# Chunked gated linear attention: one decay reference per 128-token chunk in place of one per 64-token half, and small matmuls cut to 64 stationary columns that alternate between parts of the array

## The chip, the cores and the metric

The kernel runs on one core of a Trainium2 chip. The metric is the device time of one execution in microseconds (us). TensorE (PE) does the matmuls; each is two instructions, a load of the stationary operand (LDWEIGHTS, shown as engine PEld) and a MATMUL that streams the moving operand through it. An fp32 matmul of the program is two such pairs. VectorE (DVE), ScalarE (ACT) and GpSimd (POOL) work on tiles; SyncE (SP) issues most of the loads.

## The reference

```python
batch, n_heads, seq, head_dim = (4, 8, 768, 48)
...
f = 1.0 / (1.0 + np.exp(-f_logit))
for t in range(S):
    state = f[:, :, t, :, None] * state + np.einsum('bhd,bhe->bhde', k[:, :, t], v[:, :, t])
    y[:, :, t] = np.einsum('bhd,bhde->bhe', q[:, :, t], state)
...
x = np.ascontiguousarray(attn_out.transpose(0, 2, 1, 3)).reshape(B * S, H * D)   # 3072 x 384
logits = x @ w_gate                                                              # 8 experts
...                                # greedy balanced assignment, N / E tokens for each expert
h = np.maximum(x[mask] @ w1[e], 0.0)
out[mask] = h @ w2[e]
```

## The kernel before

The program has three stages that follow each other: the attention, the assignment of tokens to experts, and the experts' FFNs. The change touches the attention alone.

A chunk is 128 tokens of one batch entry, with all 8 heads; there are 24 of them (6 in time for each of 4 batch entries, those of one time next to each other). Heads stand in pairs: a pair's two heads lie in 64 rows each (48 used) of the 128 partitions. Seven functions make the work of a chunk, and in each step of the loop each of them works on another chunk, the last function first, so that what one function needs was made a step earlier. A pool scheduler orders each engine's queue from that. Within a step, as TensorE does them:

- `gates` (L156, L158): L is the sum of the log decays from a reference token on, a 128x128 triangle against all heads; then, for each pair of heads, sums over parts of the chunk (`ind`). From L come the factors `eq`, `ek` (ACT), and from them `qg` (DVE) and `kg` (POOL).
- `gate` (L275) and `transposed` (L263): the product of finished tokens with `w_gate`, and their transposes.
- `outputs` (L244, L249): Y, the masked scores times v (`am`), plus the queries times the state before (`R`). Even and odd heads have a Y each (`par`).
- `scores` (L228): A, keys against queries; DVE copies it under the mask into `am` (L231).
- `states` (L191, L203): transposes of `qg` and `kg`, then dS, what a half adds to the state; DVE decays and adds (L182, L213).

The chunk is cut into two halves with a decay reference each. So the state is carried on twice per chunk: R0 is the state before, decayed to the first half's reference, R1 the same for the second half, and `st` the state after, each a DVE multiplication by a column of `gl`, with additions of dS between them. In L228 the stationary operand is 48x128 and in L244, L158 and L275 it is 128x128; in L203 and L249 it has 64 columns. Where an operand has at most 64 rows or columns it takes a part of the array, which its first partition and its output's first partition pick.

PSUM has 6 banks for general use and 2 for Y. Loads of a chunk are issued two chunks ahead.

Of the kernel before, what the change touches and what calls it, by code (L numbers as in the profile page):

```python
# [21 lines left out]
def kernel(  # L22
# [23 lines left out]
    """  # L46
# [9 lines left out]
    HQ = C // 4  # L56
# [25 lines left out]
    spans = const([128, NT], FP32, "spans")  # L82
# [6 lines left out]
    # wcum[s, t]: +1 for m < s <= t, -1 for t < s <= m, within a half.  # L89
# [4 lines left out]
    nc.vector.memset(mask[0:64, 64:128], 0)  # L94
    nc.vector.memset(wcum[0:64, 64:128], 0.0)
# [6 lines left out]
    ind = kept([128, 3], FP32, "ind")  # L102
    nc.vector.memset(ind[:], 0.0)
    nc.vector.memset(ind[0:32, 0:1], 1.0)
    nc.vector.memset(ind[32:64, 1:2], 1.0)
    nc.vector.memset(ind[64:96, 1:2], 1.0)
    nc.vector.memset(ind[96:128, 2:3], 1.0)

    # Buffers with parts that stay zero: a head's columns past DH, masked scores.
# [41 lines left out]
    def gates(G):  # L151
# [20 lines left out]
        gl = work.tile([128, HP, 3], FP32, name="gl", tag="gl", bufs=3)  # L172
        nc.scalar.activation(out=gl[:].rearrange("p a n -> p (a n)"),  # L173
                             in_=L[:, D:D + 3 * HP], func=AF.Exp, bias=0.0, scale=-1.0)
# [5 lines left out]
    def decayed(tag, t, gl, n, bufs):  # L180
        r = work.tile([128, HP, DH], FP32, name=tag, tag=tag, bufs=bufs)
        nc.vector.tensor_tensor(out=r[:], in0=t[:],  # L182
                                in1=gl[:, :, n:n + 1].to_broadcast((128, HP, DH)), op=ALU.mult)
        return r
# [530 lines left out]
```

## Time and profile before

| what | us |
|---|---|
| median of 3 runs | 939.6 (939.57 to 939.69) |
| span of the profiled execution | 938.4 |
| attention (first load of L156 to the end of the last L275) | 428.5 |
| assignment (442 to 665) | 223 |
| experts (675 to the end) | 263.4 |

The profiled execution's own time is its span and some 1.2 us around it, if it is taken as the median. Busy times of PE are of pipelined instructions whose ends are modelled: starts are the better measure, and the time from the first load of one group of matmuls to the first load of the next is used below as what a group takes.

### The profile page before, as it was taken

To read this page: it belongs to the slowest core of one execution; us is meant where nothing else is said; L and a number is where in the kernel's file an instruction comes from. 1 tells how busy PE (TensorE), PEld (TensorE's weight loads), DVE (VectorE), ACT (ScalarE), POOL (GpSimd) and SP (SyncE) were. 2 spreads that over 40 slices of the span, in tenths; PEclk is the share of its full clock that TensorE was granted. 3 is DMA by queue.
4 is the path that set the end of the run, shared out by engine and by line. 5 is a ranking of instruction groups with operands and counts; after the bars stand their busy time and mean duration, and the time that the engine had idled before them with its cause. 6 is when DMAs were issued, how large, how long until landed. Compare 5 with 4: busy or idle time off the path is not lost.

```text
span 938.4 us, 12159 instructions
## 1 busy us (share of the span) xinstructions
PE 747.2 (80%) x5113; PEld 589.3 (63%) x5113; DVE 318.5 (34%) x916; ACT 104.9 (11%) x249; POOL 91.4 (10%) x133
## 2 busy tenths in 40 slices
PE   4999999999999999996322233222499999999997
PEld 3889999899899899896211222211256665665654
DVE  4333323333332332322566665666401101110100
ACT  3212111121121111110000000000001111110110
POOL 4110010010010000000000000000402211210011
PEclk9999999999999999999999999999999999999999
DMA  9724232244244510000000000000323525340000
GB/s 169 116 45 83 45 76 60 51 76 127 43 125 120 193 44 11 16 9 21 2 1 1 1 1 1 1 1 1 88 89 111 184 84 176 109 160 17 8 26 25
DMA packets 118350, 59.06 MB, mean 63 GB/s; under 512 B 101649, under 2 KB 112913, under 8 KB 118289
## 3 DMA queue, kind: packets, MB, share of 16 engines
q1 hardware_dynamic: 111760, 44.06, 19.5%
q0 software_dynamic: 3072, 9.44, 2.9%
q10 hardware_dynamic: 3456, 4.72, 1.4%
q8 instruction: 42, 0.69, 0.3%
q14 instruction: 20, 0.16, 0.1%
HBM read 48.77 MB, written 9.44 MB: 62 GB/s over the span
## 4 chain that ended last, share of the span: by engine, by line
PE 21%; DVE 16%; issue 14%; POOL 2%; DMA 0%; POOLq 0%; DVEq 0%
PE H L660 7%; PE O L671 7%; PE cnt L504 5%; DVE above L496 3%; POOL out_dram L675 1%; DVE level L493 1%; PE digit L512 1%; DVE best L458 1%; DVE fills L507 1%; DVE filled L510 1%; DVE base L519 1%; POOL xe L643 1%; PE Xe L648 1%; DVE chosen L478 1%; DVE rank_incl L527 0%
## 5 line engine op out<-in xcount | busy, mean ns | idle before, releaser
L504 PE MATMUL cnt<-choice,above 128*15 128x8 bf16 x1344 | 44.5, 175 | 118.2 <-DVE above L496 118.2
L504 PEld LDWEIGHTS <-above 128*15 128x15 bf16 x1344 | 38.5, 91 | 145.1 <-DVE above L496 133.7
L660 PE MATMUL H<-xeT,w 128*128 128x384 f32 x384 | 127.3, 493 | 0.0
L671 PE MATMUL O<-w,hT 128*128 128x384 f32 x384 | 125.2, 486 | 0.0
L660 PEld LDWEIGHTS H<-xeT,w 128*128 128x128 f32 x384 | 73.7, 193 | 50.0 <-issue 2.1
L671 PEld LDWEIGHTS O<-w,hT 128*128 128x128 f32 x384 | 73.1, 190 | 50.7
L231 DVE COPY_PREDICATED am<-mask,A 128x512 f32<-128x512 int32 x48 | 34.9, 727 | 169.9 <-PE A L228 169.8
L244 PE MATMUL Y<-v,am 128*128 128x48 f32 x384 | 89.6, 408 | 0.0
L244 PEld LDWEIGHTS Y<-v,am 128*128 128x128 f32 x384 | 86.6, 331 | 2.5 <-DVE am L231 0.4
L228 PE MATMUL A<-qT,kT 48*128 48x128 f32 x384 | 74.2, 438 | 0.0
L249 PE MATMUL Y<-R,qT 48*64 48x48 f32 x704 | 71.1, 308 | 0.0
L228 PEld LDWEIGHTS A<-qT,kT 48*128 48x128 f32 x384 | 67.1, 325 | 2.1
L249 PEld LDWEIGHTS Y<-R,qT 48*64 48x64 f32 x704 | 63.2, 218 | 4.7 <-issue 0.3
L665 DVE TENSOR_SCALAR hT<-H 128x384 f32<-128x384 f32 x32 | 17.8, 558 | 122.0 <-PE H L660 106.5
L177 POOL TENSOR_TENSOR kg<-k,ek 128x384 f32<-128x384 f32 x24 | 23.9, 996 | 337.8 <-ACT gl L173 170.7
L158 PEld LDWEIGHTS L<-ind,g 128*128 128x128 f32 x192 | 46.9, 334 | 14.6 <-issue 14.3
L663 ACT ACTIVATE hT<-H 128x384 f32<-128x384 f32 x32 | 15.7, 490 | 341.8 <-PE H L660 341.8
L643 POOL DMA_INDIRECT xe<-xd,token x24 | 23.3, 971 | 284.0 <-issue 267.0
L156 PE MATMUL L<-g,wcum 128*128 128x384 f32 x48 | 39.5, 927 | 10.5 <-POOL ramp_i L399 10.5
L650 DVE COPY xeT<-Xe 128x384 f32<-128x384 f32 x24 | 12.3, 553 | 100.4 <-PE Xe L648 100.4
L675 POOL DMA_INDIRECT out_dram<-o,token x24 | 23.5, 981 | 199.6 <-ACT o L674 198.4
L158 PE MATMUL L<-ind,g 128*128 128x3 f32 x192 | 41.0, 336 | 0.0
(160 smaller groups left out, 718.9 us busy)
## 6 DMA issues: line engine op xcount, KB each, us to landing
w<-in_moe_w_dram SPq DMA_DIRECT2D x16, 1536.0 KB, 8.1
f<-in_f_logit_dram SPq DMA_DIRECT2D x24, 192.0 KB, 4.0
q<-in_q_dram SPq DMA_DIRECT2D x24, 192.0 KB, 2.9
k<-in_k_dram SPq DMA_DIRECT2D x24, 192.0 KB, 3.6
v<-in_v_dram SPq DMA_DIRECT2D x24, 192.0 KB, 3.8
xd<-x ACTq DMA_DIRECT2D x24, 192.0 KB, 1.9
xe<-xd,token POOLq DMA_INDIRECT x24, 4.5
out_dram<-o,token POOLq DMA_INDIRECT x24, 2.6
```

The lines of the kernel that those rows point to most:

```text
L156: nc.tensor.matmul(out=Lv, lhsT=wcum[:], rhs=g[:, :, 0:DH], start=True, stop=True)
L158: nc.tensor.matmul(out=L[:, D + 3 * hp:D + 3 * hp + 3], lhsT=g[:, 2 * hp:2 * hp + 2, :].rearrange("t h d -> t (h d)"), rhs=ind[:], start=T ...
L228: nc.tensor.matmul(out=A[:, 128 * hp:128 * hp + 128], lhsT=G["kT"][rows, hp, :], rhs=G["qT"][rows, hp, :], start=True, stop=True)
L231: nc.vector.copy_predicated(am[:, par], mask[:].unsqueeze(1).to_broadcast((128, HP, 128)), A[:].rearrange("s (a t) -> s a t", t=128))
L244: nc.tensor.matmul(out=Y[:, DH * hp:DH * hp + DH], lhsT=G["am"][:, par, hp, :], rhs=G["v"][:, 2 * hp + par, :], start=(hp == 0), stop=Fals ...
L249: nc.tensor.matmul(out=Y[64 * j:64 * j + 64, DH * hp:DH * hp + DH], lhsT=G["qT"][rows, hp, 64 * j:64 * j + 64], rhs=G["R"][j][rows, hp, :] ...
L496: nc.vector.tensor_tensor(out=above[:], in0=cand[:].rearrange("p (c o) -> p c o", o=1).to_broadcast((128, NT, NTH)), in1=level[:].rearrang ...
L504: nc.tensor.matmul(out=cnt[0:NTH, 0:E], lhsT=above[:, c, :], rhs=choice[:, :, c], start=(c == 0), stop=(c == NT - 1))
L643: nc.gpsimd.indirect_dma_start(out=xe[:], out_offset=None, in_=xd[:, :], in_offset=bass.IndirectOffsetOnAxis(ap=token[:, t:t + 1], axis=0))
L660: nc.tensor.matmul(out=Hp[:, 0:CAP], lhsT=w1[:, d, 128 * ft:128 * ft + 128], rhs=xT[:, d, :], start=(d == 0), stop=(d == DC - 1))
L671: nc.tensor.matmul(out=O[:, 0:D], lhsT=hT[:, ft, 128 * i:128 * i + 128], rhs=w2[:, ft, :], start=(ft == 0), stop=(ft == FC - 1))
L675: nc.gpsimd.indirect_dma_start(out=outs[t][:, :], out_offset=bass.IndirectOffsetOnAxis(ap=token[:, t:t + 1], axis=0), in_=o[:], in_offset= ...
```

## The change

The chunk has one reference, its middle, so that the state is carried on once per chunk: R is the state before times exp of minus (the sum over this chunk's first half plus the sum over the last chunk's second half), and the state after is R plus dS. The sums over halves (`ends`) come with 64 stationary columns per head. Scores, the product of the scores with v, the queries with R, dS, and the gate's product are cut into pieces of 64 stationary columns, and the loops run so that neighbours go to different parts of the array. R is made by POOL, the test for decays beyond the range reads the half sums instead of a maximum over dl. The diff, cut to the attention's functions:

```diff
-    for r in (0, 64):
-        nc.vector.tensor_scalar(
-            out=wcum[r:r + HQ, r:r + 64], in0=wcum[r:r + HQ, r:r + 64],
-            scalar1=-1.0, scalar2=None, op0=ALU.add)
+    nc.vector.tensor_scalar(out=wcum[0:64, :], in0=wcum[0:64, :],
+                            scalar1=-1.0, scalar2=None, op0=ALU.add)
...
+        ends = L[:, D:D + 2 * HP].rearrange("p (n a) -> p n a", a=HP)
         for hp in range(HP):
-            nc.tensor.matmul(
-                out=L[:, D + 3 * hp:D + 3 * hp + 3],
-                lhsT=g[:, 2 * hp:2 * hp + 2, :].rearrange("t h d -> t (h d)"),
-                rhs=ind[:], start=True, stop=True)
+            for r in range(2):
+                nc.tensor.matmul(out=ends[DP * r:DP * r + DP, :, hp], lhsT=g[:, 2 * hp + r, :],
+                                 rhs=ind[:], start=True, stop=True)
...
-        nc.vector.tensor_reduce(out=spans[:, G["i"]:G["i"] + 1],
-                                in_=dl[:].rearrange("t h d -> t (h d)"), axis=AX_X, op=ALU.max,
-                                apply_absolute_value=True)
...
+        span = spans[:, G["i"]]
+        nc.vector.tensor_copy(out=span, in_=ends)
+
+        if G["c"]:
+            gl = work.tile([128, HP], FP32, name="gl", tag="gl", bufs=3)
+            nc.gpsimd.tensor_tensor(out=gl[:], in0=span[:, 0], in1=spans[:, G["i"] - B, 1],
+                                    op=ALU.add)
+            nc.scalar.activation(out=gl[:], in_=gl[:], func=AF.Exp, bias=0.0, scale=-1.0)
...
-        R0 = decayed("R0", state[b], gl, 0, 4) if c else None
-        R1 = decayed("R1", added(0, R0), gl, 1, 4)
-        G["R"] = (R0, R1)
-        if not last:
-            state[b] = decayed("st", added(1, R1), gl, 2, B + 1)
+        R = None
+        if c:
+            R = work.tile([128, HP, DH], FP32, name="R", tag="R", bufs=5)
+            nc.gpsimd.tensor_tensor(
+                out=R[:], in0=state[b][:],
+                in1=G["gl"][:].unsqueeze(2).to_broadcast((128, HP, DH)), op=ALU.mult)
...
+        dS = ps("dS")
+        for hp in range(HP):
+            for r in range(2):
                 nc.tensor.matmul(
-                    out=dS[j][r:r + DP, DH * hp:DH * hp + DH],
-                    lhsT=G["kg"][64 * j:64 * j + 64, h, :],
-                    rhs=v_[64 * j:64 * j + 64, h, :], start=True, stop=True)
+                    out=dS[DP * r:DP * r + DP, DH * hp:DH * hp + DH],
+                    lhsT=G["kg"][:, 2 * hp + r, :], rhs=v_[:, 2 * hp + r, :],
+                    start=True, stop=True)
...
+        A = [ps("A") for _ in range(2)]
+        for hp in range(HP):
+            for j in range(2):
+                for par in range(2):
+                    rows = slice(DP * par, DP * par + DH)
+                    nc.tensor.matmul(
+                        out=A[par][HC * j:HC * j + HC, 128 * hp:128 * hp + 128],
+                        lhsT=G["kT"][rows, hp, HC * j:HC * j + HC],
+                        rhs=G["qT"][rows, hp, :], start=True, stop=True)
         for par in range(2):
-            A = ps("A")
-            rows = slice(DP * par, DP * par + DH)
-            for hp in range(HP):
-                nc.tensor.matmul(out=A[:, 128 * hp:128 * hp + 128],
-                                 lhsT=G["kT"][rows, hp, :], rhs=G["qT"][rows, hp, :],
-                                 start=True, stop=True)
...
+        Y = [ps("Y", "sum") for _ in range(2)]
+        for hp in range(HP):
+            for par in range(2):
+                for j in range(2):
+                    nc.tensor.matmul(
+                        out=Y[par][HC * j:HC * j + HC, DH * hp:DH * hp + DH],
+                        lhsT=G["am"][:, par, hp, HC * j:HC * j + HC],
+                        rhs=G["v"][:, 2 * hp + par, :],
+                        start=(hp == 0), stop=False, skip_group_check=True)
+        if G["R"] is not None:
+            for hp in range(HP):
+                for j in range(2):
+                    for par in range(2):
+                        rows = slice(DP * par, DP * par + DH)
+                        nc.tensor.matmul(
+                            out=Y[par][HC * j:HC * j + HC, DH * hp:DH * hp + DH],
+                            lhsT=G["qT"][rows, hp, HC * j:HC * j + HC],
+                            rhs=G["R"][rows, hp, :],
+                            start=False, stop=True, skip_group_check=True)
...
         for d in range(DC):
-            nc.tensor.matmul(out=X[:, D:D + E], lhsT=G["xT"][:, d, :], rhs=wg[:, d, :],
-                             start=(d == 0), stop=(d == DC - 1))
+            for j in range(2):
+                half = slice(HC * j, HC * j + HC)
+                nc.tensor.matmul(out=X[half, D:D + E], lhsT=G["xT"][:, d, half], rhs=wg[:, d, :],
+                                 start=(d == 0), stop=(d == DC - 1))
```

TensorE's queue in one step in the middle of the attention before, from L on; the count behind x is of the program's matmuls, and the size is that of the output:

```order
L156 MATMUL L<-g_94,wcum 128x384
L158 MATMUL L<-ind,g_94 128x3 x4
L275 MATMUL X<-wg,xT 128x8 x3
L263 MATMUL X<-ident,x 128x128 x3
L244 MATMUL Y<-v,am_104 128x48 x4
L249 MATMUL Y<-R_610,qT 64x48 x4
L249 MATMUL Y<-R_614,qT 64x48 x4
...
L228 MATMUL A<-qT,kT 128x128 x8
L191 MATMUL T<-ident,qg_97 128x128 x4
L191 MATMUL T<-ident,kg_100 128x128 x4
L203 MATMUL dS<-v,kg_100 64x48 x16
```

(The three rows of Y stand twice, once for each `par`.) The same step of the changed kernel:

```order
L151 MATMUL L<-g_91,wcum 128x384
L155 MATMUL L<-ind,g_91 64x2 x8
L277 MATMUL X<-wg,xT 64x8 x6
L263 MATMUL X<-ident,x 128x128 x3
L237 MATMUL Y<-v,am_98 64x48 x16
L247 MATMUL Y<-R,qT 64x48 x16
L220 MATMUL A<-qT,kT 64x128 x16
L183 MATMUL T<-ident,qg_94 128x128 x4
L183 MATMUL T<-ident,kg_97 128x128 x4
L202 MATMUL dS<-v,kg_97 64x48 x8
```

The order of the groups stays. Y is no longer made in two rounds, the full-width run of L, its sums, gate, transposes and Y is cut by pieces of 64 columns, L247 and L220 stand next to each other with parts of 64 rows by 64 columns, and dS has half as many matmuls, of 128 rows.

DVE's queue in one step before, where the state is carried on:

```order
L182 TENSOR_TENSOR R_846<-st,gl 128x192
L231 COPY_PREDICATED am_105<-mask,A 128x512 x2
L196 COPY kT<-T 128x512
L213 TENSOR_TENSOR ssum<-dS,R_846 128x192
L182 TENSOR_TENSOR R_850<-ssum,gl 128x192
L213 TENSOR_TENSOR ssum<-dS,R_850 128x192
L165 TENSOR_SCALAR dl<-L 128x384
L182 TENSOR_TENSOR st<-ssum,gl 128x192
L167 TENSOR_REDUCE spans<-dl 128x1
L176 TENSOR_TENSOR qg_98<-q,eq 128x8x48
```

and in the changed kernel:

```order
L225 COPY_PREDICATED am_98<-mask,A 128x512 x2
L188 COPY kT<-T 128x512
L209 TENSOR_TENSOR st<-dS,R 128x192
L160 TENSOR_SCALAR dl<-L 128x384
L165 COPY spans<-L 128x8
L279 COPY logits<-X 128x8
L266 COPY xT<-X 128x384
L174 TENSOR_TENSOR qg_93<-q,eq 128x8x48
```

Five of DVE's operations on 128x192 become one, the reduction becomes a copy of 128x8, and `qg` stands behind the copies of X instead of ahead of them.

## Rows read from the trace of the kernel before

**Rows 1.** The page: span, and granted TensorE clock in 40 slices.

```profile
span 938.4 us, 12159 instructions
...
PEclk9999999999999999999999999999999999999999
```

**Rows 2.** Busy time of each engine from the attention's first L156 to its last L275.

```profile
core 0: us, PE busy (x) PEld busy (x) DVE busy (x) ACT busy (x) POOL busy (x), PEclk, DMA share, GB/s
10.47:438.97 428.50, 425.62 (x2826) 385.81 (x2826) 138.62 (x298) 74.88 (x189) 37.42 (x56) 1.00 0.33 75
```

**Rows 3.** Waits, 60 to 400 us: total us, times, longest.

```profile
DVE am L231 <- PE A L228: 146.0, 37, 7.6
...
PEld dS L203 <- ACT qT L196: 1.0, 3, 0.3
```

**Rows 4.** Timeline of weight loads, one middle step: start, duration, group of loads.

```profile
201.63 0.50 PEld L156 LDWEIGHTS L<-g,wcum 128*128 128x128 f32 x2
...
208.30 1.39 PEld L249 LDWEIGHTS Y<-R,qT 48*64 48x64 f32 x16
209.78 1.78 PEld L244 LDWEIGHTS Y<-v,am 128*128 128x128 f32 x8
211.65 1.39 PEld L249 LDWEIGHTS Y<-R,qT 48*64 48x64 f32 x16
213.13 2.80 PEld L228 LDWEIGHTS A<-qT,kT 48*128 48x128 f32 x16
216.16 0.71 PEld L191 LDWEIGHTS T<-ident,qg 128*128 128x128 f32 x4 [0.22 <-issue]
216.85 0.87 PEld L191 LDWEIGHTS T<-ident,kg 128*128 128x128 f32 x4
218.05 1.41 PEld L203 LDWEIGHTS dS<-v,kg 64*64 64x64 f32 x32 [0.33 <-issue]
219.55 0.50 PEld L156 LDWEIGHTS L<-g,wcum 128*128 128x128 f32 x2
```

**Rows 5.** Timeline of matmuls from 201.63, the full-width run of that step.

```profile
201.63 1.65 PE L156 MATMUL L<-g,wcum 128*128 128x384 f32 x2
203.07 1.71 PE L158 MATMUL L<-ind,g 128*128 128x3 f32 x8
204.64 1.43 PE L275 MATMUL X<-wg,xT 128*128 128x8 f32 x6
205.92 0.88 PE L263 MATMUL X<-ident,x 128*128 128x128 f32 x3
```

**Rows 6.** Timeline of weight loads in an early step, whose L249 has one half.

```profile
25.40 1.78 PEld L244 LDWEIGHTS Y<-v,am 128*128 128x128 f32 x8 [0.22 <-DVE am L231]
27.27 0.93 PEld L249 LDWEIGHTS Y<-R,qT 48*64 48x64 f32 x8
28.29 0.71 PEld L191 LDWEIGHTS T<-ident,qg 128*128 128x128 f32 x4
```

**Rows 7.** L660 in the first expert, two stretches: us, PE busy (x), granted clock.

```profile
676.48:680.25 3.77, 3.77 (x7) 1.00 0.55 158
680.28:693.48 13.20, 13.20 (x42) 1.00 0.08 25
```

**Rows 8.** Engines in one middle step (columns as in rows 2).

```profile
219.55:237.47 17.92, 17.92 (x125) 16.30 (x124) 5.92 (x14) 2.75 (x7) 1.00 (x1) 1.00 0.26 58
```

**Rows 9.** Groups by line and form: us in all, mean ns, idle before.

```profile
L177 POOL TENSOR_TENSOR kg<-k,ek 128x384 f32<-128x384 f32 x24 | 23.9, 996 | 337.8 <-ACT gl L173 170.7 <-issue 167.1
...
L165 DVE TENSOR_SCALAR dl<-L 128x384 f32<-128x384 f32 x24 | 13.4, 558 | 60.2 <-PE L L158 60.2
...
L170 ACT ACTIVATE eq<-dl 128x384 f32<-128x384 f32 x24 | 12.5, 521 | 35.7 <-DVE dl L165 34.4 <-ACT x L253 0.5
...
L182 DVE TENSOR_TENSOR R<-st,gl 128x192 f32<-128x192 f32 x20 | 7.6, 379 | 0.0
...
L277 DVE COPY logits<-X 128x8 f32<-128x8 f32 x24 | 4.1, 172 | 13.3 <-PE X L275 13.3
```

**Rows 10.** Timeline, the first chunk: TensorE's first transposes.

```profile
15.94 1.09 PE L191 MATMUL T<-ident,qg 128*128 128x128 f32 x4 [2.32 <-DVE qg L176]
```

More of the change, by code (lines that the diff above doesn't have):

```diff
@@ L55 @@
     HP = H // 2
-    HQ = C // 4
+    HC = C // 2
     DC = D // 128
@@ L81 @@
     xd = dram.tile([N, D], FP32, name="xd")
[L82 removed]
+    spans = const([128, NT, 2, HP], FP32, "spans")
     attn = ExitStack()
@@ L166, in gates @@
                                 op0=ALU.min, op1=ALU.max)
[L167 to L169 removed]
         nc.scalar.activation(out=eq[:], in_=dl[:], func=AF.Exp, bias=0.0, scale=-1.0)
         nc.scalar.activation(out=ek[:], in_=dl[:], func=AF.Exp, bias=0.0, scale=1.0)
[L172 to L174 removed]
+        span = spans[:, G["i"]]
[5 more added lines that the diff above has]
+            nc.scalar.activation(out=gl[:], in_=gl[:], func=AF.Exp, bias=0.0, scale=-1.0)
+            G["gl"] = gl
         qg, kg = q_bufs[i], k_bufs[i]
@@ L177, in gates @@
         nc.gpsimd.tensor_tensor(out=kg[:, :, 0:DH], in0=G["k"][:], in1=ek[:], op=ALU.mult)
-        G.update(gl=gl, qg=qg, kg=kg)
[L180 to L184, printed above, removed]
+        G.update(qg=qg, kg=kg)
     def states(G):
-        b, c, gl, v_ = G["b"], G["c"], G["gl"], G["v"]
+        b, c, v_ = G["b"], G["c"], G["v"]
         for nm, t, copy in (("qT", G["qg"], nc.scalar.copy), ("kT", G["kg"], nc.vector.tensor_copy)):
@@ L196, in states @@
             copy(out=G[nm][:].rearrange("p a t -> p (a t)"), in_=T[:])
-        last = c == NCH - 1
-        dS = [ps("dS") for _ in range(1 if last else 2)]
-        for j in range(len(dS)):
-            for h in range(H):
-                hp, r = h // 2, DP * (h % 2)
-                nc.tensor.matmul(
-                    out=dS[j][r:r + DP, DH * hp:DH * hp + DH],
-                    lhsT=G["kg"][64 * j:64 * j + 64, h, :],
-                    rhs=v_[64 * j:64 * j + 64, h, :], start=True, stop=True)
@@ L208, in added @@
-        def added(j, t):
-            d = dS[j][:, 0:HP * DH].rearrange("p (a e) -> p a e", e=DH)
-            if t is None:
-                return d
-            s = work.tile([128, HP, DH], FP32, name="ssum", tag="ssum", bufs=3)
-            nc.vector.tensor_tensor(out=s[:], in0=d, in1=t[:], op=ALU.add)
-            return s[:]
-        R0 = decayed("R0", state[b], gl, 0, 4) if c else None
-        R1 = decayed("R1", added(0, R0), gl, 1, 4)
-        G["R"] = (R0, R1)
-        if not last:
-            state[b] = decayed("st", added(1, R1), gl, 2, B + 1)
+        R = None
@@ L222, in scores @@
+        d = dS[:, 0:HP * DH].rearrange("p (a e) -> p a e", e=DH)
+        state[b] = work.tile([128, HP, DH], FP32, name="st", tag="st", bufs=B + 2)
+        if c:
+            nc.vector.tensor_tensor(out=state[b][:], in0=d, in1=R[:], op=ALU.add)
+        else:
+            nc.vector.tensor_copy(out=state[b][:], in_=d)
     def scores(G):
         am = a_bufs[G["i"] % NB]
-        for par in range(2):
-            A = ps("A")
-            rows = slice(DP * par, DP * par + DH)
-            for hp in range(HP):
-                nc.tensor.matmul(out=A[:, 128 * hp:128 * hp + 128],
-                                 lhsT=G["kT"][rows, hp, :], rhs=G["qT"][rows, hp, :],
-                                 start=True, stop=True)
+        A = [ps("A") for _ in range(2)]
@@ L238, in outputs @@
         x = work.tile([128, D], FP32, name="x", tag="x", bufs=3)
-        halves = [j for j in range(2) if G["R"][j] is not None]
-        for par in range(2):
-            Y = ps("Y", "sum")
-            rows = slice(DP * par, DP * par + DH)
-            for hp in range(HP):
-                nc.tensor.matmul(out=Y[:, DH * hp:DH * hp + DH],
-                                 lhsT=G["am"][:, par, hp, :], rhs=G["v"][:, 2 * hp + par, :],
-                                 start=(hp == 0), stop=False, skip_group_check=True)
-            for j in halves:
-                for hp in range(HP):
-                    nc.tensor.matmul(
-                        out=Y[64 * j:64 * j + 64, DH * hp:DH * hp + DH],
-                        lhsT=G["qT"][rows, hp, 64 * j:64 * j + 64], rhs=G["R"][j][rows, hp, :],
-                        start=False, stop=True, skip_group_check=True)
+        Y = [ps("Y", "sum") for _ in range(2)]
[17 more added lines that the diff above has]
+                            start=False, stop=True, skip_group_check=True)
+        for par in range(2):
             nc.scalar.copy(
                 out=x[:].rearrange("t (a r d) -> t r a d", r=2, d=DH)[:, par],
-                in_=Y[:, 0:HP * DH].rearrange("t (a d) -> t a d", d=DH))
+                in_=Y[par][:, 0:HP * DH].rearrange("t (a d) -> t a d", d=DH))
         row = S * b + C * c
@@ L303 @@
     span = const([128, 1], FP32, "span")
-    nc.vector.tensor_reduce(out=span[:], in_=spans[:], axis=AX_X, op=ALU.max)
+    nc.vector.tensor_reduce(out=span[:], in_=spans[:].rearrange("p c n a -> p (c n a)"), axis=AX_X,
+                            op=ALU.max)
     nc.vector.tensor_scalar(out=span[:], in0=span[:], scalar1=LIMIT, scalar2=None, op0=ALU.is_ge)
```

15 lines of the change are left out of this document (7 added, 8 removed).

## The prediction

> **What bounds the kernel now.** I read the page first, for the stages. The attention runs from 10.47 to 438.97 us, and there TensorE is busy 425.6 of 428.5 us, all other engines under a third of it [rows 2]. A busy PE need not be a PE that waits for nobody, so I looked at the waits of the stage: the others wait for TensorE (DVE's masked copy of A alone 146 us), and the most that TensorE waits for another engine is 1.0 us in 340 [rows 3]. A middle step repeats at 17.92 us to the hundredth, which says the same: TensorE's queue sets the pace and nothing else does. Only what shortens this queue shortens the kernel, and nearly all of it comes out at the end, since the assignment begins when the last logits are there.
>
> Next, what in the queue takes the time. In the full-width run, six L275 with 8 moving columns take 204.64 to 205.92, 0.213 us each, and three transposes with 128 columns 0.22 each [rows 5]: what is streamed hardly matters, the load of 128 stationary columns does. L156 is the one exception: 1.44 us for two instructions of 384 moving columns [rows 5]. If a load is some 0.16 of it, a stream of 384 columns is 0.64 us, 1.67 ns a column; 48 columns are 0.080 us and 128 are 0.213.
>
> A group ends with a gap. Eight loads of 128 columns take 1.87 us (25.40 to 27.27), eight of 64 columns into one part of the array 1.02 [rows 6]. With 0.213 a load the first is 1.707 + 0.163; with half of that, 0.107, the second is 0.853 + 0.164. So **a load of 64 columns costs 0.107 us in its part, and a group that is shaped otherwise than its neighbour 0.163 on top**.
>
> Do parts work at the same time? In a step, dS has 32 loads of 64 columns in 1.50 us (218.05 to 219.55) [rows 4]. One after the other they would take 32 x 0.107 + 0.16 = 3.58. Its neighbours alternate between two column parts: two at a time is 1.87. The rest comes from its second half, which uses the other 64 rows, starting while the first half still runs; four parts overlap there. L249 fills one part with 8 loads before it goes on to the next: 16 loads in 1.48 against 1.87 one by one [rows 4]. L228 has 16 loads of 128 columns and 128 moving columns in 3.02 against 3.58 [rows 4]; there two row parts overlap, streams included. What alternates overlaps; what comes in runs does so only where runs meet.
>
> The clock has to be known, since all these are times of one level of it. The page grants 1.00 throughout [rows 1], but the same 384-column matmul of the first expert starts every 0.64 us (six starts in 3.77) and from 680.3 on every 0.32 (41 starts in 13.20), both at a printed 1.00 [rows 7]. The first is the lower level (1.2 GHz), and L156's 0.64 puts the attention there too. I take the attention's prices as they stand, at 1.2 GHz.
>
> **The change, part by part.** A middle step of the queue, price by price; "per part" counts the loads that one part of the array gets.
>
> - L151, now alone between groups of other shape: 0.16 + 2 x 0.64 + 0.17 for the end = 1.61.
> - L155 and L277 (16 and 12 loads of 64 columns, two column parts, one shape): 14 x 0.107 + 0.16 = 1.66. Before, 14 full loads cost 2.99.
> - L263, three transposes alone: 3 x 0.213 + 0.19 = 0.83 (0.19 as in T, whose 8 take 1.90 [rows 4]).
> - L237, 32 loads, two parts: 16 x 0.107 + 0.16 = 1.87. Before 16 full loads, 3.41.
> - L247 and L220, one shape with four parts: L247 8 x 0.107 per part; L220 has 128 moving columns, so that the stream of 0.213 sets its pace and not the load: 8 x 0.213; and 0.23 for the end of a longer stream. Together 2.79, before 2 x 1.48 + 3.02.
> - T as before, 1.90. L202, 16 loads, two parts: 8 x 0.107 + 0.16 = 1.02, before 1.50.
>
> A middle step is 11.68 us instead of 17.92. Over the stage: L151 24 x 1.61 = 38.6; L155 and L277 336 x 0.107 + 29 x 0.163 = 40.6; L263 19.9; L237 44.9; L220 41.0, L247 (20 chunks have a state before them) 17.1, their ends 25 x 0.23 = 5.8; T 45.5; L202 (20 chunks) 20.3. Sum 273.7. To it come the first chunk's wait for `qg` (2.32 before [rows 10]; shorter L155 brings it forward with the wait, so about 1.7 stays) and some 0.6 at the end, less 1 for three places where T and L stand next to each other: 275. That is **153.5 us less than 428.5**. From the span of 938.4 [rows 1] this gives 784.9; what lies around the span, 1.2 us, makes 786.
>
> What I cost at nothing, with its cover. DVE loses the reduction, three multiplications and one addition, and gets a copy like L277's 0.17 [rows 9]: from 5.9 us a step [rows 8] to about 4.3, in a step of 11.7. POOL gets R, between DVE's 0.38 for that size and its own 1.00 for twice the size [rows 9], and the addition for `gl`, under that; with `kg` 1.00 and the clamp it comes to some 2.3 a step. The path that could show is from the end of L155: dl 0.56, eq and ek 0.52 each, kg 1.00 [rows 9], 2.6 in all, then R on POOL behind `kg`. The transposes of kg come 0.6 (L277) + 0.8 + 1.9 + 2.8 + 0.9 = 7.0 us behind L155. `qg`, now queued on DVE behind the copies of X, is made 2 us ahead of its transposes or more. R is read by L247 a step later. If the cover were gone, a step would wait for the rest of 2.6 + 0.5 at most: with a queue twice as fast it still fits. The two A now finish together, so that L151, which takes a bank of theirs, waits for the first masked copy: 0.73 behind A, with 2.9 us of T and dS ahead of L151.
>
> Prices not in the trace: pieces of 128 rows by 64 columns (L155, L277, L237, L202) stand in no row. Lower bound: two parts at a time as in dS, 0.053 a piece; upper bound: one by one, 0.107 as in rows 6. I take the lower, since dS differs only in its rows. Four streams of 128 columns at a time: L228 shows two, dS four of 48. I take four (0.053 a piece), upper bound two (0.107).
>
> The Trainium skill, "TensorE: Matmul & The Clock Gate", Part 3, says that a load overlaps running matmuls only where the row groups differ. dS's two column parts share their rows and overlap, and L275's full loads follow each other at the load's own 0.213 with streams in between, so the trace speaks against it. Its result is the third rival below.
>
> **The rivals.**
>
> - *Four streams don't run together.* L220 goes at two pieces of 0.213 at a time: 24 x 8 x 0.213 = 41 us more, 827.
> - *128-row pieces don't overlap.* 1760 of them at 0.107 instead of 0.053: 94 more, 880.
> - *Slower: pieces on the same rows run strictly one after another, load, then stream.* A piece of L237 or L202 then costs 0.107 + 0.080, of L155 0.110, of L277 0.120. L237 + 103, L202 + 43, L155 and L277 + 41: 187 more, 973. It becomes a loss when a 128-row piece costs over 0.053 + 153/1760 = 0.14 us. That loads before are not lengthened by streams (rows 5) speaks against it.
> - *The clock rises.* The new queue packs the same products into two thirds of the time. What raised the clock in the trace was 4.4 us of full-width 384-column streams [rows 7]; 428 us of a busy TensorE with small matmuls did not. At the upper level TensorE's 275 us halve to 137, and with fill and the other engines' 4.3 us a step the stage takes some 150: 661. If it rises late or falls again, anything between that and 786. The same page of the Trainium skill, in "What's actually happening", says that activity releases the clock; by that rule the attention before should already have run at 2.4 GHz, and rows 5 and 7 show that it did not.
>
> **How the numbers follow.** The forecast as summed has 0.53, and its own range is 776 to 797: 2 us for the place where the first expert's clock rises, the rest for ends of groups (175 of them, 0.05 each). Four streams not together 0.12; 128-row pieces not together 0.07; strictly one after another 0.05; the clock 0.22, of which about half below 690; within 0.2% (about what a measurement of this kernel can tell from no change) 0.01. The range of 690 to 835 holds the forecast, the first rival and the late rises: 0.53 + 0.12 + 0.11, and part of mixtures. Faster 0.94, same 0.01, slower 0.05.
>
> **What would show it.** In the timeline of loads of the changed kernel: L237 x32 takes 1.87 (3.6 if the parts don't overlap, 6 if strictly one by one); L247 and L220 together 2.8 (4.5 with two streams); a step 11.7, the same to a hundredth. Waits of TensorE for DVE or POOL near zero. L151's two instructions 0.64 apart; 0.32 would be the clock. If the step changes from one to the next, another engine has become the bound and the sum is wrong in its cover.

## The result, and the profile after

The changed kernel takes 676.6 us (median of 4 runs, 675.3 to 679.3), the kernel before 939.6 on the same chip: ratio 0.720 [0.719, 0.722]. The forecast was 786 with a range of 690 to 835. It was too slow by 109 us and the range missed; the last of its rivals, the rising clock, came about.

The page of the changed kernel, span and granted clock in 40 slices (against [rows 1]):

```profile
span 675.2 us, 13443 instructions
...
PEclk9999999998755555555555556999999999999999
```

The attention now fills the first ten slices, the assignment the 5s, the experts the rest. This trace records when the clock changes between its lower level (1.2 GHz) and its upper one (2.4 GHz): up at 26.67 us, down at 149.55, up at 156.37, down at 176.85 when the assignment begins, up at 415.79 in the experts. Its windows (columns as in [rows 2]): the whole attention first, then a stretch at the upper level, the second one at the lower, and one middle step at the upper.

```profile
9.95:175.80 165.85, 161.22 (x3482) 129.42 (x3482) 94.98 (x214) 71.97 (x185) 50.95 (x96) 0.98 0.79 193
26.60:149.50 122.90, 121.55 (x2789) 98.34 (x2789) 75.41 (x172) 59.13 (x153) 41.52 (x74) 1.00 0.87 214
149.50:156.40 6.90, 6.90 (x98) 5.40 (x94) 2.80 (x5) 1.12 (x3) 1.13 (x2) 0.51 0.65 231
...
66.56:72.99 6.43, 6.43 (x157) 5.25 (x153) 3.92 (x9) 3.51 (x9) 2.64 (x5) 1.00 0.86 182
```

The attention takes 166 us instead of 428.5 [rows 2]; assignment and experts together are as long as they were. TensorE is still busy nearly all the time (161.2 of 165.9 us), so it still sets the pace. The printed clock before a trace's first recorded change reads 1.00 at either level (in the kernel before, the whole attention does [rows 1]), so the durations decide. Here are the weight loads of the changed kernel: a step at the lower level, a piece of the second lower stretch, and the middle step at the upper level (columns as in [rows 4]).

```profile
17.98 0.50 PEld L151 LDWEIGHTS L<-g,wcum 128*128 128x128 f32 x2
19.56 0.94 PEld L155 LDWEIGHTS L<-ind,g 128*64 128x64 f32 x16 [1.08 <-issue]
20.52 1.58 PEld L220 LDWEIGHTS A<-qT,kT 48*64 48x64 f32 x32
22.46 0.72 PEld L183 LDWEIGHTS T<-ident,qg 128*128 128x128 f32 x4 [0.36 <-issue]
...
24.36 0.94 PEld L202 LDWEIGHTS dS<-v,kg 128*64 128x64 f32 x16 [0.33 <-issue]
25.38 0.50 PEld L151 LDWEIGHTS L<-g,wcum 128*128 128x128 f32 x2
...
150.23 0.94 PEld L247 LDWEIGHTS Y<-R,qT 48*64 48x64 f32 x32
151.04 1.63 PEld L220 LDWEIGHTS A<-qT,kT 48*64 48x64 f32 x32
153.00 0.71 PEld L183 LDWEIGHTS T<-ident,qg 128*128 128x128 f32 x4 [0.33 <-issue]
...
67.62 0.55 PEld L202 LDWEIGHTS dS<-v,kg 128*64 128x64 f32 x16 [0.17 <-issue]
68.22 0.30 PEld L151 LDWEIGHTS L<-g,wcum 128*128 128x128 f32 x2
69.06 0.55 PEld L155 LDWEIGHTS L<-ind,g 128*64 128x64 f32 x16 [0.55 <-issue]
...
70.46 1.01 PEld L237 LDWEIGHTS Y<-v,am 128*64 128x64 f32 x32 [0.17 <-issue]
71.53 0.56 PEld L247 LDWEIGHTS Y<-R,qT 48*64 48x64 f32 x32
71.99 0.87 PEld L220 LDWEIGHTS A<-qT,kT 48*64 48x64 f32 x32
73.03 0.20 PEld L183 LDWEIGHTS T<-ident,qg 128*128 128x128 f32 x2 [0.17 <-issue]
```

From start to start: dS (L202) takes 1.02 at the lower level and 0.60 at the upper, A (L220) 1.94 and 1.04. What stays between the halves is the end of a group. Sixteen pieces of dS, two at a time, are 8 x 0.107 = 0.85 at the lower level and 0.43 at the upper; 0.17 is left over at both. So the loads halve and the ends do not, and a step is 6.43 us instead of half of 11.68.

The waits of the changed kernel, 60 to 145 us (columns as in [rows 3]), and behind them POOL's wait for `f` in the kernel before, 60 to 400 us:

```profile
DVE am L225 <- PE A L220: 20.3, 13, 1.6
...
POOL f L141 <- DMA f<-in_f_logit_dram: 9.7, 4, 5.3
...
PEld T L183 <- POOL kg L175: 1.0, 2, 0.5
```

```profile
POOL f L146 <- DMA f<-in_f_logit_dram: 15.2, 2, 11.4
```

DVE waits for TensorE, as before, and TensorE waits for POOL 1.0 us in 85. POOL's wait for the transfer of `f` comes four times in 85 us, where it came twice in 340: at this pace the transfers, 0.86 of the DMA engines' time in the step above, begin to show.

### The profile page after: what moved, and what is told of

The parts are those of the page before. It is cut to its first block, busy times and chain, and to the rows that moved or that the text cites. A ratio compares the mean times of both kernels' runs of the same rounds, so it can differ in the third digit from the quotient of the medians.

```text
span 675.2 us, 13443 instructions
## 1 busy us (share of the span) xinstructions
PE 481.7 (71%) x5769; PEld 332.5 (49%) x5769; DVE 274.6 (41%) x827; ACT 101.9 (15%) x245; POOL 104.9 (16%) x173
## 4 chain that ended last, share of the span: by engine, by line
PE 29%; DVE 22%; issue 19%; POOL 2%; DMA 0%; POOLq 0%; DVEq 0%
PE H L663 10%; PE O L674 9%; PE cnt L507 7%; DVE above L499 4%; POOL out_dram L678 2%; DVE level L496 2%; PE digit L515 1%; DVE best L461 1%; DVE fills L510 1%; DVE filled L513 1%; DVE base L522 1%; PE Xe L651 1%; POOL xe L646 1%; DVE chosen L481 1%; DVE rank_incl L530 1%
## 5 line engine op out<-in xcount | busy, mean ns | idle before, releaser
L225 DVE COPY_PREDICATED am<-mask,A 128x512 f32<-128x512 int32 x48 | 32.4, 729 | 34.8 <-PE A L220 34.8
L151 PE MATMUL L<-g,wcum 128*128 128x384 f32 x48 | 24.3, 593 | 10.0 <-POOL ramp_i L402 10.0
L677 ACT COPY o<-O 128x384 f32<-128x384 f32 x24 | 11.5, 478 | 128.1 <-PE O L674 128.1
L499 DVE TENSOR_TENSOR above<-hi,level 128x360 bf16<-128x360 f32 x56 | 29.8, 532 | 1.2
L510 DVE TENSOR_TENSOR fills<-cnt,wanted 15x8 f32<-15x8 f32 x56 | 8.6, 153 | 50.0 <-PE cnt L507 50.0
L237 PE MATMUL Y<-v,am 128*64 128x48 f32 x768 | 27.8, 226 | 0.0
L220 PE MATMUL A<-qT,kT 48*64 48x128 f32 x768 | 27.7, 285 | 0.0
L237 PEld LDWEIGHTS Y<-v,am 128*64 128x64 f32 x768 | 24.7, 139 | 3.9 <-issue 3.7
L515 PE MATMUL digit<-filled,ones 15*128 15x1 bf16 x56 | 9.0, 161 | 24.1 <-DVE filled L513 24.1
L160 DVE TENSOR_SCALAR dl<-L 128x384 f32<-128x384 f32 x24 | 13.4, 558 | 27.7 <-PE L L155 27.7
```

The costliest lines, as they stand in the source:

```text
L220: nc.tensor.matmul(out=A[par][HC * j:HC * j + HC, 128 * hp:128 * hp + 128], lhsT=G["kT"][rows, hp, HC * j:HC * j + HC], rhs=G["qT"][rows, ...
L225: nc.vector.copy_predicated(am[:, par], mask[:].unsqueeze(1).to_broadcast((128, HP, 128)), A[par][:].rearrange("s (a t) -> s a t", t=128))
L237: nc.tensor.matmul(out=Y[par][HC * j:HC * j + HC, DH * hp:DH * hp + DH], lhsT=G["am"][:, par, hp, HC * j:HC * j + HC], rhs=G["v"][:, 2 * h ...
L499: nc.vector.tensor_tensor(out=above[:], in0=cand[:].rearrange("p (c o) -> p c o", o=1).to_broadcast((128, NT, NTH)), in1=level[:].rearrang ...
```

## The experiments

Fifteen kernels, in three groups by what they ask. Differences between kernels are differences of medians; all of them ran beside the kernel before (939.3 to 939.6). Where nothing else is said, "upper" and "lower" are what the trace's recorded changes of the level say.

### Which part of the change raises the clock?

**Pieces, two references.** The kernel before with its sums (shown), A, Y, R and gate cut to 64 columns and alternating as in the change, and dS's four parts in turn.

```diff
...
-                lhsT=g[:, 2 * hp:2 * hp + 2, :].rearrange("t h d -> t (h d)"),
...
+            for r in range(2):
...
+                    lhsT=g[:, 2 * hp + r, :], rhs=ind[:], start=True, stop=True)
...
```

> The kernel before with its two references, its small matmuls cut to 64 stationary columns that alternate (A, Y, R, the sums, the gate's product; dS with all four parts in turn). If the density of the queue is what raises the clock, the one reference is not needed: L156's second stream takes 0.32 us for most of the attention, a step about 6.5 us, total 680 to 700 (DVE keeps its 5.9 us a step and may show). If the saved work of the one reference is needed for the rise: a step of 11.7 us at 0.64, total about 786.

693.0 (688.1 to 694.8; a fourth execution took 703.9), ratio 0.738 [0.737, 0.740]. The upper level holds from 24.5 to 92.8 and from 103.0 to 188.4:

```profile
24.60:92.70 68.10, 64.63 (x1628) 52.10 (x1626) 55.18 (x124) 33.73 (x87) 18.53 (x24) 1.00 0.92 197
103.10:188.30 85.20, 81.00 (x2049) 65.92 (x2047) 65.15 (x153) 30.38 (x82) 14.24 (x14) 1.00 0.61 172
```

The steps in which nothing waits take 6.43 to 6.44, as in the changed kernel: the second reference costs TensorE nothing there. The profiled execution, 688.1, is 11 us over that of the changed kernel (677.0). Later steps of 7.0 to 10.9 us hold them: in most of these TensorE stands idle for about 1 us, and the longest is in the stretch at the lower level.

**One reference alone.** The change without the pieces in sums, A (shown), Y, R and gate; dS stays, since one reference changes it anyway.

```diff
...
-                        lhsT=G["kT"][rows, hp, HC * j:HC * j + HC],
...
+                                 lhsT=G["kT"][rows, hp, :], rhs=G["qT"][rows, hp, :],
...
```

> The one reference alone: the sums, A, Y and the gate's product in the shapes and order of before; only dS has 16 loads in place of 32. If the density raises the clock: it stays at the lower level, a step is 17.92 - 0.48 = 17.4 us, total about 930. If the one reference is what matters: 0.32 us for 384 columns, a step of some 9 us, total about 740.

884.6 (876.0 to 886.0), 0.938 [0.934, 0.943]. Nine of its steps take 17.45, which the lower level's prices give (17.4); the others, around nine short rises between 17.95 and 352 us, take 8 to 16.

```profile
21.40:80.00 58.60, 58.60 (x349) 52.29 (x350) 21.15 (x42) 14.97 (x36) 11.68 (x18) 0.56 0.44 94
```

In this window the level rises twice, at 38.43 and 62.32, and is lost again 3.4 us later each time, although TensorE is busy throughout.

**Pieces without alternation.** The change, with each group's pieces in runs that stay in one part of the array.

```diff
-        for hp in range(HP):
+        for par in range(2):
             for j in range(2):
-                for par in range(2):
+                for hp in range(HP):
...
```

> The changed kernel with the same 64-column pieces, the loops turned so that pieces follow each other in one part of the array and change part only between runs. If alternation is what makes the pieces overlap and the density what raises the clock: the lower level, a step of 18 to 20 us, total 940 to 990, slower than before. If pieces of 64 columns are enough: within 3% of the changed kernel, about 680.

748.0 (745.3 to 751.4), 0.796 [0.793, 0.798]. The upper level holds from 31.0 to 249.5, with a step of 9.78.

```profile
31.10:249.40 218.30, 216.80 (x3357) 190.87 (x3356) 95.63 (x203) 68.68 (x172) 46.11 (x81) 1.00 0.51 129
```

My theory that a queue must be packed to raise the clock fell in this form: alternation is worth 71 us, but not through the level.

**A push at the start.** The kernel before, with 7 dense matmuls of 384 columns while TensorE waits for the first inputs.

```diff
+    def dense(n):
+        for _ in range(n):
+            W = ps("W", "sum")
+            nc.tensor.matmul(out=W[:, 0:384], lhsT=burst[:, 0:128], rhs=burst[:], start=True,
+                             stop=True)
...
+    dense(7)
```

> The kernel before with 7 dense 128x384 matmuls in TensorE's first 10 idle us, so that the clock can rise before the first chunk. If the density of the queue decides the level all the time: it falls back within some us and the time is 935 to 940. If a rise lasts whatever the queue holds, as long as TensorE is busy: L156's streams at 0.32 through the attention, a step of some 9.2 us, total about 730.

939.5 (938.7 to 940.2), 1.000 [0.999, 1.001]. Its matmuls, and a later window:

```profile
10.32 0.88 PE L166 MATMUL L<-g,wcum 128*128 128x384 f32 x2 [2.75 <-POOL ramp_i L409]
11.04 1.61 PE L168 MATMUL L<-ind,g 128*128 128x3 f32 x8
...
11.20:40.00 28.80, 25.71 (x172) 22.87 (x171) 9.94 (x19) 7.74 (x19) 4.62 (x10) 0.50 0.91 134
```

The push works: the first two 384-column streams take 0.72 together, where [rows 5] have 1.44. From 11.14 on the level is the lower again, and steps are 17.92; in the whole attention the level is not won back. The fall comes in the first chunk, behind a pause of 2.75 us, and the first steps of the changed kernel lose a push as well (below). So this run does not show whether a middle step of the kernel before would keep a level that it is given.

**One group in pieces: A, or Y and R.** The kernel before, with only these groups as in the change.

> The kernel before with A alone in pieces that alternate over four parts. At the lower level A takes 1.94 us instead of 3.02 and the total is about 914; at the upper level a step of some 9.3 us, total about 735. If one group raises the clock, and that is A with its 128 moving columns: near 735. If it takes several groups in pieces, since the level follows how much of the time streams run: near 914, with short rises at most.

A alone: 846.2, 849.4, 872.2 and 879.6 in four executions, too far apart for a ratio. The profiled one, 846.2, has fourteen rises of 3 to 14 us and steps of 7.8 to 16.6 us.

> The kernel before with Y alone in pieces (masked scores times v, and queries times R, which alternate over four parts). At the lower level 3.4 us less a step, total about 860; at the upper level a step of some 8 us, total about 705. If Y is the group that raises the clock: near 705. If it takes several groups: between, nearer 860.

Y and R alone: 858.9 (857.7 to 859.3), 0.914 [0.913, 0.916]. But for 3.4 us at 354 it stays at the lower level, so that its loads show the pieces' prices there:

```profile
203.98 1.79 PEld L244 LDWEIGHTS Y<-v,am 128*64 128x64 f32 x32 [0.33 <-issue]
205.86 0.95 PEld L253 LDWEIGHTS Y<-R,qT 48*64 48x64 f32 x32
206.90 2.80 PEld L228 LDWEIGHTS A<-qT,kT 48*128 48x128 f32 x16
```

Y takes 1.88 (forecast 1.87), R 1.04, and the step 14.43 (14.5 expected).

**One group taken back: A, Y, or sums and gate.** The changed kernel, with the group as it was before.

> The changed kernel with A in the shape and order of before (48x128, one row part after the other). Lower level: a step of 12.9 us, total about 816. Upper level: about 7.1, total about 693. If A alone raises the clock: near 816. If several groups do: near 693.

A back: 689.0 (688.5 to 689.5), 0.734 [0.732, 0.735]; upper from 27.96 to 188.4, step 7.19.

> The changed kernel with Y in the shape and order of before (128x128 masked scores, R's products in runs). Lower level: a step of 15.2 us, total about 868. Upper level: about 8.4, total about 723. If Y's full-width loads, with 0.080 us of stream in 0.213, are what kept the clock down: near 868. If what is left in pieces is enough: near 723.

Y back: 737.8 (735.4 to 740.4), 0.785 [0.783, 0.788]; the level changes every 3 to 20 us from 55 on, steps 7.5 to 11.1.

> The changed kernel with the decay sums and the gate in their old shape: 8 and 3 loads of 128x128 with 2 and 8 streamed columns, instead of 16 and 6 pieces. If only the prices change, the clock stays at the upper level and a step grows from 6.4 us by about 0.55 us (8 x 0.107 + 0.15 = 1.0 against 0.46 for the sums, 0.48 against 0.46 for the gate): 676.6 + 24 x 0.55 = 690 us. If a stretch of 1.4 us in which TensorE loads and hardly streams lets the clock fall, it changes level often in the attention as it did when Y was full-width: 720 to 760 us. If the clock never rises: the 786 us that the lower level's prices give, and 0.9 us per step on top, about 808.

Sums and gate back: 681.9 (680.7 to 682.8), 0.725 [0.724, 0.727]; upper from 26.66 to 180.3 without a break, step 6.88. So fourteen full loads with 2 or 8 streamed columns in each step did not end the upper level here.

### Is it the form of the loads, or what is streamed?

**The kernel before, with more columns streamed.** Every load, shape and order as it was; 96 columns are streamed instead of 3 in the sums, 48 in Y and 8 in the gate, and the additional ones go where nothing reads them.

```diff
-    ind = kept([128, 3], FP32, "ind")
+    ind = kept([128, 96], FP32, "ind")
...
-                                 lhsT=G["am"][:, par, hp, :], rhs=G["v"][:, 2 * hp + par, :],
...
+                twice = G["v"][:, 2 * hp + par, :].unsqueeze(1).to_broadcast((128, 2, DH))
...
+                                 lhsT=G["am"][:, par, hp, :], rhs=twice,
...
+                             rhs=wg[:, d, :].unsqueeze(1).to_broadcast((128, 96 // E, E)),
...
```

> The kernel before with every shape and every load as it was, but more streamed columns where loads had hidden hardly any: 96 instead of 3 in the decay sums, 96 instead of 48 in Y, 96 instead of 8 in the gate; the additional columns are not read by anything. At the lower level 96 columns take 0.16 us (384 take 0.64), which the load of 0.213 beside them hides. Theory that the amount streamed per time decides the level: the clock rises and a kernel that does more work is faster, 730 to 760 us if it holds through the attention (step 17.9 to about 9.4), 850 to 900 if it comes and goes. Rival, that the form of the loads decides (64 columns at a time, changing part): nothing rises, 939 to 945 us.

771.9 us (770.1 to 773.7; a fourth execution, of 1961.8, is left out of the median and the ratio and stays unexplained), 0.821 [0.819, 0.822]. A kernel that does strictly more work is 167 us faster. Its windows, the first upper stretch, the lower one behind it, and one step:

```profile
27.70:130.10 102.40, 102.40 (x1251) 92.75 (x1251) 67.46 (x133) 35.95 (x90) 22.72 (x26) 1.00 0.70 174
130.20:140.30 10.10, 10.10 (x72) 8.85 (x70) 4.60 (x10) 3.05 (x7) 0.06 (x1) 0.50 0.62 202
...
103.22:113.13 9.91, 9.91 (x127) 9.00 (x124) 6.58 (x14) 3.16 (x8) 1.92 (x2) 1.00 0.95 266
```

The shortest middle steps take 9.91 us instead of 17.92 [rows 8], those around a stretch at the lower level 12.2 to 12.4. After 130 us the level comes and goes while TensorE is busy without a gap (10.10 of 10.10).

**Y back, with more columns streamed.** As the run at 737.8, with Y's 48 columns streamed twice.

```diff
...
-                nc.tensor.matmul(out=Y[:, DH * hp:DH * hp + DH],
+                nc.tensor.matmul(out=blocks[:, hp:HP + 1:HP - hp],
-                                 lhsT=G["am"][:, par, hp, :], rhs=G["v"][:, 2 * hp + par, :],
+                                 lhsT=G["am"][:, par, hp, :], rhs=twice,
...
```

> The changed kernel with Y in full-width loads as in the run that undid the outputs (737.8 us, levels changing every few us), and 96 instead of 48 streamed columns in Y, the additional ones read by nothing. Theory that the streamed amount decides: the upper level holds, every step takes the 7.5 us that the shortest steps of that run took: 700 to 723 us, with more work than in the run at 738. Rival, that full-width loads in a queue of pieces make the level fall: 738 us or more.

711.9 (711.0 to 713.8), 0.758 [0.757, 0.759]. Windows with 48 columns (the run at 737.8), and then with 96 (this one):

```profile
24.30:55.00 30.70, 30.70 (x469) 25.87 (x465) 17.30 (x40) 13.88 (x35) 9.30 (x16) 1.00 0.69 148
55.10:61.80 6.70, 6.70 (x73) 5.74 (x74) 2.39 (x4) 1.95 (x4) 0.54 (x2) 0.50 0.55 122
```

```profile
55.00:212.00 157.00, 155.66 (x2530) 134.30 (x2528) 72.26 (x165) 54.41 (x136) 36.55 (x66) 1.00 0.58 152
67.28:75.70 8.42, 8.42 (x142) 7.21 (x138) 4.06 (x10) 3.61 (x9) 2.13 (x4) 1.00 0.55 110
```

The upper level holds to the end of the attention. A step is 8.42, where I had expected the 7.5 of the other run's shortest; that one stands at the attention's end, where groups are missing. The time still falls by 26 us.

**The changed kernel, with fewer columns streamed.** All loads and pieces stay; half of the scores and of the outputs are left out.

```diff
-                        rhs=G["qT"][rows, hp, :], start=True, stop=True)
+                        rhs=G["qT"][rows, hp, 0:64], start=True, stop=True)
...
-                        rhs=G["v"][:, 2 * hp + par, :],
+                        rhs=G["v"][:, 2 * hp + par, 0:24],
...
```

> The changed kernel with every load, piece and order as it is, but half the streamed columns in A (64 of 128), Y and R (24 of 48); the missing half of the columns is filled with a copy of the computed one, so half of the scores and outputs are left out. Theory that the streamed amount holds the level: less work and a longer time; levels change within the attention, 700 to 740 us, or the lower level throughout, about 762 us (786 less 24 x 1.0 for A). Rival, that the form of the pieces holds it: the upper level stays, and A saves up to 0.5 us per step: 664 to 677 us.

678.5 (676.5 to 686.4), 0.724 [0.720, 0.728].

```profile
22.30:25.60 3.30, 3.30 (x22) 2.10 (x22) 1.05 (x2) 1.42 (x3) 0.37 (x1) 0.50 0.96 192
29.10:42.70 13.60, 13.51 (x146) 10.07 (x144) 6.08 (x15) 4.04 (x9) 2.44 (x4) 0.50 0.56 125
42.80:151.90 109.10, 106.75 (x2672) 87.77 (x2671) 72.18 (x197) 54.41 (x143) 39.74 (x71) 1.00 0.79 190
```

A draw between the theories. The level rose twice for 3.4 us, at 18.82 and 25.64, and fell again before it stayed, at 42.71 instead of 26.67; a step that is 0.43 shorter (6.00) made up for that and no more. But from 42.7 on it held with half the columns in three groups.

### What bounds it next, and a faster version

**Pushes.** The changed kernel with 7 dense matmuls at the start and 6 while the first gather flies.

```diff
+    dense(7)
...
+    nc.vector.tensor_copy(out=burst[:, 0:NT], in_=token[:])
+    dense(6)
     xTs = {0: gather(0)}
```

> The changed kernel with 7 dense 128x384 matmuls while TensorE waits for the first inputs, and 6 more after the last place is known, while the first gather flies. Theory, that from its first step on the changed queue holds a level that it is given: the steps that ran at the lower level until 26.67 us run at the upper one, about 6 us less there, and the first transposes and matmuls of the experts, at the lower level until 415.79, save 3 us: 667 us. Rival, that the first steps (with gaps for inputs and a part of the groups missing) lose the level as the kernel before lost it: 673 us. Rival, that the pause between burst and work undoes both: 676 us.

671.8 (670.7 to 677.1), 0.717 [0.714, 0.719]. The first steps lost the level at 13.54, as the rival said, and won it back at 23.78; in the experts the upper level holds from 402.66 on, where the changed kernel has it from 415.79.

**Pushes, and fewer changes of shape.** dS and the new state get a function of their own, `added`, and a step goes through the functions in this order (beside each, how many chunks it stands behind the newest):

```diff
+    order = ((outputs, 4), (scores, 3), (transposed, 5), (states, 2), (gates, 1), (added, 2),
+             (gate, 5), (decays, 0))
```

> As the run with both bursts, and the groups of a step put in an order in which the load shape changes 3 times instead of 7: sums, dS, gate and Y (128x64 pieces), then R and A (64x64), then X, both T and the cumulative sums (128x128). Theory, that each change costs a drain of about 0.15 us at the upper level: 4 x 0.15 x 24 = 14 us less than the run with bursts, about 653 us. Rival, that sums, dS, gate and Y in a row, some 2.4 us with few streamed columns, let the clock fall: levels change within the attention, 690 to 750 us. Rival, that the drain depends on something other than the shape: no difference to the run with bursts.

668.1 (667.4 to 671.6), 0.712 [0.711, 0.714].

```profile
30.00:78.00 48.00, 48.00 (x1229) 41.61 (x1225) 32.82 (x77) 27.06 (x71) 18.77 (x35) 1.00 0.91 194
78.00:100.00 22.00, 19.73 (x472) 16.61 (x471) 13.69 (x31) 11.33 (x28) 8.28 (x16) 1.00 0.97 225
100.00:136.00 36.00, 32.73 (x835) 28.00 (x836) 22.48 (x52) 15.78 (x41) 10.62 (x19) 1.00 1.01 282
```

The step is 5.85, 0.58 less than 6.43; four fewer ends were to give 0.6. Of the 14 us that this makes over 24 steps only 4 came out. From 78 us on TensorE has gaps and the DMA engines are full: the experts' first weights are issued from 93 us on, among the inputs.

**The weights later.** The same, with the first three experts' weights made to wait for the attention's end.

```diff
+            nc.vector.tensor_copy(out=w1[0:1, 0, 0:1], in_=hits[0:1, 0:1])
...
         nc.sync.dma_start(out=w1[:], in_=moe_w1[e].rearrange("(c p) f -> p c f", p=128))
...
```

> As the run with both bursts and grouped shapes, and the first three experts' weights are loaded after the attention instead of from 93 us on. That run's steps are 5.85 us until 74 us, and seven of the later ones 6.2 to 9.4, with the DMA engines' share at 0.97 to 1.01 and waits behind f, q, k and v; one of these pauses comes ahead of a fall of the clock. Theory that the weights take the transfers' place: the seven steps come down to 5.85, 10 us less, about 658 us. Rival, that the inputs alone fill the DMA engines (0.91 already before the weights): 2 to 4 us less, about 665 us. Rival, that the experts wait for their weights: over 670 us.

663.5 (662.5 to 667.3), 0.707 [0.705, 0.709]: the fastest version, 13 us under the changed kernel. The three windows of the run before, again:

```profile
30.00:78.00 48.00, 46.88 (x1188) 40.27 (x1180) 31.92 (x73) 26.21 (x69) 19.20 (x36) 1.00 0.93 197
78.00:100.00 22.00, 20.69 (x500) 17.34 (x492) 14.51 (x31) 11.86 (x29) 8.48 (x16) 1.00 0.90 192
100.00:136.00 36.00, 36.00 (x955) 31.38 (x954) 24.48 (x57) 16.69 (x44) 10.48 (x20) 1.00 0.46 106
```

From 87 us on all steps are 5.86 or less, and the upper level lasts to 158.65. Slow steps remain ahead of that (7.09, 6.76 and 6.71 us), where the inputs alone take 0.90 to 0.93 of the DMA engines; the gain of 4.6 us lies between theory and rival.

## Why the prediction was wrong

**The step that failed** is "I take the attention's prices as they stand, at 1.2 GHz". It carries prices from a queue at the lower level to another queue, as if the level did not depend on the queue. The runs showed in its place that the changed queue spends 142 of its 166 us at the upper level, with a middle step of 6.43 us where the forecast has 11.68. The evidence for the step, that 428 us of a busy TensorE with small matmuls did not raise the clock, was read too coarsely. The rows showed the difference [rows 5, 6]: in those 428 us TensorE mostly loads. The gate's matmuls stream 8 columns each behind 0.213 us of load, and Y's 48. The experts' matmuls that raised the clock [rows 7] stream all the time. Pieces of half the width stream the same columns behind half the load, and with parts side by side the same columns in less time.

The run with wide streams separates the form of the loads from what is streamed behind them. Nothing but columns was added to the kernel before, no load became shorter, and the attention ran mostly at the upper level. Y with 96 columns instead of 48 shows it a second time, for one group. So it is shown that more columns behind the same loads are enough in this kernel; that the streamed columns are all there is to it is not, since the run with half of A's, Y's and R's columns held the level in the middle of the attention. What these runs exclude as the reason: that one reference is gone (the level holds with two, too, and with one reference alone it only rises nine times for a few us), and the alternation (it holds without). A alone, or Y and R alone, in pieces are not enough.

The Trainium skill, "TensorE: Matmul & The Clock Gate", section "What's actually happening", has activity release the clock. The forecast set this aside because a TensorE that the profile calls busy stayed at the lower level. The runs do not contradict the page, but they show that the profile's busy time is not the thing to read it by: the kernel before (425.6 of 428.5 us busy) and the wide run's first upper stretch (102.4 of 102.4) are both busy and stand at different levels.

**The other steps held.** At the lower level, where the changed kernel runs until 26.67, the sum's terms are: L151 1.58 (forecast 1.61) and its neighbour L155 0.96, L220 alone 1.94 (8 x 0.213 + 0.23), T 1.90, L202 1.02 (1.02); from 150.23 to 153.00 L247 and L220 together 2.77 (2.79); in the run with only Y and R cut, Y 1.88 (1.87). So four streams do run side by side, pieces of 128 rows do overlap in two column parts, and the three rivals against that are out. Two figures that the prediction gives for the groups before are prices and not readings: 14 full loads at 2.99 took 2.85 in [rows 5] (203.07 to 205.92), and Y's 16 at 3.41 take 1.87 for each eight in [rows 4], with the ends. Its sum does not use them.

Of the 786, then, 109 us are the clock. The rival's own figure of 661 was 16 too low. It took the stage at 150, and 166 were measured. To TensorE's 137 come the stretches at the lower level, 16.7 us at the start and 6.8 from 149.55, which cost about half their length, 12 us, more than the upper level would; and the ends of groups, which do not halve: 6.43 less 5.84 is 0.59 a step, 12 us over the 20 steps at the upper level. That is 161. The 5 left were not traced one by one; waits such as that for `f` above are among them.

The Trainium skill, on the same page, "Single matmul latency", has the tail of a single bf16 matmul drain in about the same time at both levels, 175 ns. The rows of dS, an fp32 group, agree in size, with 0.17 at both; that the end of a group is this drain no run here shows.

**Covers.** DVE has 3.92 us in a step (4.3 forecast), POOL 2.64 (2.3), ACT 3.51. The groups of the changed kernel that answer to [rows 9]:

```profile
L175 POOL TENSOR_TENSOR kg<-k,ek 128x384 f32<-128x384 f32 x24 | 25.6, 1066 | 27.2 <-ACT ek L163 21.4 <-issue 4.0 <-DMA v<-in_v_dram 0.7
...
L193 POOL TENSOR_TENSOR R<-st,gl 128x192 f32<-128x192 f32 x20 | 10.3, 517 | 0.0
...
L279 DVE COPY logits<-X 128x8 f32<-128x8 f32 x24 | 4.0, 167 | 2.9 <-PE X L277 2.9
```

R on POOL is 0.52, between the bounds of 0.38 and 1.00. The claim that the cover fits "with a queue twice as fast" held to the 1.0 us above. What I had not looked at as a cover is the DMA engines: 0.33 busy in the attention before [rows 2], they are at 0.79 in the changed one and at 0.86 in its middle step, and they bound the next version.

**Where the gain is.** One reference with dS's shape takes 0.47 off a lower-level step (17.92 to 17.45) and nothing off TensorE's step at the upper level. Alternation takes 71 us. The pieces are what brings this queue to the upper level for good.

**What stays open.** The runs do not show what makes the level change at the moment at which it does. In the changed kernel the fall at 149.55 follows a pause of 0.70 us in the gate's matmuls, but the run with Y back and the wide run fall with no pause at all, and the run with grouped shapes pauses for 1.72 us at 84 us without a fall. It costs some 3 us. Where the level rose in the first steps without a push, it did so at 18 to 31 us; in the versions of the change a push was lost again while TensorE waited for the first `qg`.

## What to carry to other kernels

Where TensorE is busy with loads of many stationary columns for few moving ones, look which clock level the durations show before pricing a change: cutting such loads into narrower pieces for parts of the array brought the upper level here, on top of the overlap, and then everything else on the queue gets faster too. Price such a change at both levels, and let the range hold both. When a queue becomes more than twice as fast, list the transfers among its covers; here the DMA engines went from 0.33 to 0.79 of the attention, and moving the weights out of the inputs' way was worth as much (4.6 us) as the last improvement of the queue (3.8).

## What was not expected of the hardware

- More streamed columns behind unchanged loads made a kernel faster: 939.4 to 771.9 us.
- A TensorE that the profile shows busy without a gap falls to the lower level (at 55.02 with Y taken back, at 130.12 with wide streams) and rises again.
- The end of a group that is shaped otherwise than its neighbour takes 0.17 us at both levels, so a change of shape weighs twice as much at the upper one: four fewer per step took 0.58 off 6.43.
